# An attention and routed-expert kernel on one core: P transposes on 64-row tiles, wider copies out of PSUM, output scaled on GpSimd

## The chip, the cores and the metric

The kernel runs on one NeuronCore of a Trainium2 chip. The core has five engines that run side by side, each through its own instructions in order: TensorE (PE in the profile, with PEld for the loads of its stationary operand), VectorE (DVE), ScalarE (ACT), GpSimd (POOL) and SyncE (SP, which here issues most of the DMAs). TensorE writes to PSUM, an accumulator memory that DVE and ACT read; GpSimd works on SBUF in this kernel. The metric is the device time of one execution in microseconds. A profiled execution gives a span from the first to the last instruction and the time of each instruction in it.

## The reference, cut to what matters

```python
# q, k, v: 4 batches x 8 heads x 576 positions x 64, float32
scores = 0.125 * q @ k.T
thresh = max(scores, axis=-1) - tau
scores = where(scores >= thresh, scores, -1e9)
attn = exp(scores - max(scores)); attn /= attn.sum(-1) + 1e-9
x = (attn @ v) rearranged to 2304 tokens x 512
# then two layers on the tokens
gate, expert = softmax and argmax of cosine(x, expert_emb) / tau_moe     # 8 experts
x = gate * (relu(x @ w1[expert]) @ w2[expert])                          # 512 -> 1024 -> 512
h = x @ w_in; out = (h * tanh(softplus(h))) @ w_out                     # 512 -> 2048 -> 512
```

Only the attention part is touched by the change; the two layers behind it take two thirds of the time.

## The kernel before, in words

A planner (class `Plan`) takes every piece of work with an engine, a duration, what it reads and writes, and a priority, and writes out one order for each engine. The priorities are sums of a piece's place in the loop and of numbers in the table `PR` (line 34). The order is fixed when the kernel is built; at run time each engine goes through its own list and waits on semaphores.

The attention runs over 16 pairs of heads. For a pair, `scores` makes nine units: unit u = 0 to 7 holds 128 queries of one head against 576 keys, unit 8 holds the last 64 queries of both heads. A unit goes PE (L502), row maximum on DVE (L506), threshold on POOL (L507), exponential on ACT (L508), then mask, product and row sum on DVE (L509), which writes P to SBUF. The scores have a contraction of 64, so each unit uses the array as two tiles of 64 rows and 128 columns: keys 0 to 287 on the upper rows, 288 to 575 on the lower ones, each into its own PSUM bank.

`transp` turns P around for the second product. For each of nine key tiles c of 128 keys, four transposes of 128x128 (L526) fill one PSUM bank, and ACT copies the bank to SBUF (L532, 512 columns). `transp_last` does the same for unit 8 (five transposes at L545, one copy of 640 columns at L548). `pv` multiplies with V in five steps a = 0 to 4 (L561); V is the stationary operand, 64 columns wide, so that the two heads use the two column halves of the array at the same time. Step 4 takes key tile 4, which holds keys of both heads, 64 rows each, on four tiles of 64x64. ACT copies the sum to `osb` (L572, L573); PE turns it back (L583, 5 transposes of 128x128) and forms the logits (L585, 5 products with 16 columns of the matrix `EB`); DVE scales both by the reciprocal row sum and writes `xs` and `xl` to SBUF (L589, L590). After four pairs a batch is done and `router` runs: small DVE steps, a rank by PE (L646 to L649), five squared sums on ACT (`junk`, L675), writes of x to DRAM.

All of this shares four PSUM tiles of two banks each, named D (`two`, line 279): a unit of scores holds one from PE's first product until DVE's L509 is through, two key tiles share one, and the output of `pv` (called `ox` in the code) holds one from the first step until its scaled form is out.

Near the end of the attention `early` picks the largest expert from the first three batches (L714 on PE, then DVE, then L744), so that its weights and its first two tiles of tokens can be fetched (POOL L955) before the last batch is routed. The expert stage follows (L1017 turns the fetched tokens, L1041 and L1059 multiply), then the last layer (L1255, L1283).

## Time and profile before

| | us |
|---|---|
| median of 3 runs | 1044.64 (1043.76 to 1044.7) |
| the profiled execution, own time | 1041.71 |
| its span | 1039.8 |
| PE busy | 987.2 (95%) |
| PEld busy | 797.9 (77%) |
| DVE busy | 757.5 (73%) |
| ACT busy | 548.2 (53%) |
| POOL busy | 321.3 (31%) |
| mean granted TensorE clock | 0.973 of full speed |

The span falls into stages with different limits, so the shares above are averages over unlike things. The attention takes the first third. The columns of the views that follow: a stretch of the windows view gives, for each engine, the time busy and in brackets the number of instructions, then the granted TensorE clock, the share of the DMA engines and GB/s. A row of the timeline gives start, length, engine, line, operation, output<-inputs, shape (rows x columns of the array, then the operand) and count, with idle time and its releaser in square brackets. Matmuls overlap each other, so the length of a row holds the latency of its last one; the distance from one row's start to the next row's start is what the engine took. An fp32 product has two records in the trace, a transpose has one.

### The profile page before, as it was taken

The numbers are of one execution on the slowest core, as the hardware profiler recorded it, in microseconds if no ns is written. First come the engines' busy times: TensorE is split into PE (matmuls) and PEld (weight loads), VectorE is DVE, ScalarE is ACT, GpSimd is POOL, SyncE is SP. The second block draws the span as 40 slices with busy tenths as digits, with TensorE's granted clock in tenths as the row PEclk, the third lists the DMA queues.
The fourth block names the chain that finished last, engine by engine and source line by source line (L and its number), as shares of the span: only waits on it lengthen the run. The fifth ranks groups of instructions, "written<-read, shape, count | busy, mean of one in ns | idle before, by whom it ended". The sixth has DMA issues, their size and how long they took to land. (4 is left out here: it accounts for less than half of the span.)

```text
span 1039.8 us, 16987 instructions
## 1 busy us (share of the span) xinstructions
PE 987.2 (95%) x6381; PEld 797.9 (77%) x6381; DVE 757.5 (73%) x1104; ACT 548.2 (53%) x932; POOL 321.3 (31%) x446
## 2 busy tenths in 40 slices
PE   6999999999898979999999978999999999999996
PEld 3555655655565869899999867998999989899985
DVE  6787887887775858566777859978586866758670
ACT  3666766766654535445566536563544545354440
POOL 4222222212211232322441637423333232422341
PEclk7999999999999789999999988999999999999999
DMA  8222321322313787677799563001000010100000
GB/s 256 82 69 73 119 84 59 119 77 65 100 39 105 264 285 273 234 266 254 266 319 340 185 212 127 22 11 31 22 21 31 22 31 11 32 21 1 22 20 21
DMA packets 41818, 119.28 MB, mean 115 GB/s; under 512 B 8768, under 2 KB 8768, under 8 KB 37632
## 3 DMA queue, kind: packets, MB, share of 16 engines
q1 hardware_dynamic: 37168, 103.13, 29.7%
q0 software_dynamic: 4560, 14.99, 4.4%
q8 instruction: 52, 0.85, 0.4%
q14 instruction: 38, 0.31, 0.1%
HBM read 91.04 MB, written 27.06 MB: 114 GB/s over the span
## 5 line engine op out<-in xcount | busy, mean ns | idle before, releaser
L1273 DVE RECIPROCAL b<-p 128x512 f32<-128x512 f32 x72 | 239.3, 3339 | 18.4 <-ACT p L1270 17.1
L506 DVE TENSOR_REDUCE m<-D 128x1 f32<-128x576 f32 x144 | 107.3, 755 | 50.1 <-PE D L502 48.0
L1276 POOL TENSOR_TENSOR lo<-c,hi 128x512 fp32r<-128x512 f32 x72 | 93.2, 1301 | 139.9 <-ACT hi L1275 133.6
L502 PE MATMUL D<-QK 64*128 64x288 f32 (+1 forms) x640 | 110.8, 468 | 15.1 <-DVE P L509 8.1
L508 ACT ACTIVATE E<-D,m 128x576 f32<-128x576 f32 x144 | 104.7, 745 | 36.5 <-DVE m L506 34.8
L509 DVE SCALAR_TENSOR_TENSOR P<-D,thr,E 128x576 f32<-128x576 f32 x128 | 101.9, 812 | 6.6 <-ACT E L508 3.7
L1268 ACT ACTIVATE p<-S 128x512 f32<-128x512 f32 x72 | 43.0, 598 | 119.3 <-PE S L1255 107.7
L507 POOL TENSOR_SCALAR thr<-m,ntau 128x1 f32<-128x1 f32 x144 | 38.7, 269 | 215.6 <-DVE m L506 193.8
L1274 DVE SCALAR_TENSOR_TENSOR c<-b,S 128x512 f32<-128x512 f32 x72 | 46.4, 658 | 71.0 <-POOL lo L1276 71.0
L1041 PE MATMUL S<-xh,wh 128*128 128x256 f32 (+1 forms) x288 | 89.3, 310 | 0.5 <-ACT xh L1023 0.4
L1041 PE MATMUL S<-xl,wh 128*128 128x256 f32 (+1 forms) x288 | 88.5, 307 | 0.5 <-DVE xl L1024 0.5
L1041 PE MATMUL S<-xh,wl 128*128 128x256 f32 (+1 forms) x288 | 88.3, 307 | 0.0
L526 PE MATMUL D<-ident,P 128*128 128x128 f32 x576 | 84.0, 285 | 2.5 <-ACT hi L532 1.8
L526 PEld LDWEIGHTS D<-ident,P 128*128 128x128 f32 x576 | 63.7, 145 | 28.8 <-issue 10.7
L949 DVE TENSOR_TENSOR wl<-raw,wh 128x1024 fp32r<-128x1024 f32 x49 | 59.4, 1231 | 36.0 <-ACT wh L947 35.5
L1255 PE MATMUL S<-hi,wl 128*128 128x256 f32 x288 | 81.5, 283 | 0.0
L1255 PE MATMUL S<-hi,wh 128*128 128x256 f32 x288 | 81.5, 283 | 0.0
L1255 PE MATMUL S<-lo,wh 128*128 128x256 f32 x288 | 81.4, 283 | 0.0
L561 PE MATMUL D<-hi,V 128*64 128x512 f32 (+1 forms) x160 | 76.5, 616 | 4.0 <-issue 3.8
L1275 ACT CAST hi<-c 128x512 fp32r<-128x512 f32 x72 | 44.1, 618 | 63.6 <-PE B L1283 49.5
L561 PE MATMUL D<-lo,V 128*64 128x512 f32 (+1 forms) x160 | 76.5, 617 | 0.0
L502 PEld LDWEIGHTS D<-QK 64*128 64x128 f32 (+1 forms) x640 | 45.5, 183 | 37.3 <-issue 12.2
(246 smaller groups left out, 2553.1 us busy)
## 6 DMA issues: line engine op xcount, KB each, us to landing
raw<-in_wm_dram SPq DMA_DIRECT2D x32, 1024.0 KB, 6.3
QK<-in_qk_dram SPq DMA_DIRECT2D x32, 432.0 KB, 4.2
fraw<-in_w_in_dram SPq DMA_DIRECT2D x16, 512.0 KB, 6.1
fraw<-in_w_out_dram SPq DMA_DIRECT2D x16, 512.0 KB, 5.2
V<-in_v_dram SPq DMA_DIRECT2D x16, 480.0 KB, 3.4
y_dram<-osb SPq DMA_DIRECT2D x21, 257.0 KB, 5.3
x_dram<-xs SPq DMA_DIRECT2D x16, 256.0 KB, 5.0
w_in_dram<-c SPq DMA_DIRECT2D x16, 256.0 KB, 6.3
```

The source lines that it names most:

```text
L502: nc.tensor.matmul(o, lhsT=QK()[r, a, q0:q0 + w], rhs=QK()[r, a, S:], start=True, stop=True)
L506: add("DVE", 755, lambda: nc.vector.tensor_reduce(m(), sv(), axis=AX.XY, op=ALU.max, negate=True), r=[sc], w=[m], prio=at + PR["max"])
L508: add("ACT", 755, lambda: nc.scalar.activation(Ev(), sv(), AF.Exp, bias=m(), scale=1.0), r=[sc, m], w=[E], prio=at + PR["exp"])
L509: add("DVE", 893, lambda: nc.vector.scalar_tensor_tensor(outs[0]().rearrange("p (a b) -> p a b", a=2), sv(), thr(), Ev(), op0=ALU.is_ge, o ...
L526: pd(nc.tensor.transpose(pt()[:, i * 128:(i + 1) * 128], Ps[i]()[:, c * 128:(c + 1) * 128], self.ident))
L561: mul = lambda j, o, r, c, rhs: nc.tensor.matmul(o, lhsT=V1()[r, c, :], rhs=rhs, start=(a == 0), stop=(a == 4))
L949: add(le, d, lambda: e.tensor_tensor(lo()[:, s], raw()[:, s], hi()[:, s].bitcast(F32), op=ALU.subtract), r=[kr, kh], w=[kl], prio=prio + .5)
L1041: hd(nc.tensor.matmul(hp().rearrange("p (k n) -> p k n", n=128), lhsT=a()[:, kc, f], rhs=x()[:, k0:k0 + n, kc * 128:(kc + 1) * 128], start ...
L1255: hd(nc.tensor.matmul(hp()[:, f * 256:(f + 1) * 256], lhsT=w, rhs=x, start=(n == 0), stop=(n == 11)))
L1273: add("DVE", 3270, lambda q_=q_, r_=r_: v.reciprocal(r_(), g2(q_)), r=[q_], w=[r_], prio=au + R["rc"])
L1274: add("DVE", t_dve(512), lambda gg=gg, r_=r_, hp=hp, hd=hd: hd(v.scalar_tensor_tensor(gg(), r_(), -0.5, hp(), op0=ALU.add, op1=ALU.mult)), ...
L1276: add("POOL", t_pool(512), lambda gg=gg, gh=gh, gl=gl: g.tensor_tensor(g2(gl), gg(), g2(gh).bitcast(F32), op=ALU.subtract), r=[gg, gh], w= ...
```

## The change

1. P's transposes use 64-row tiles. A 128x128 block of P becomes two transposes of 64 rows by 128 columns, upper and lower half of the queries, each into its own PSUM bank: the same two row tiles that the scores use. The transposes of unit 8, those of the output and the logit products are split in the same way.
2. Two key tiles c share one PSUM tile of two banks and one ACT copy of 1024 columns takes both out; the ninth key tile has a copy of 512. A pair then has five such copies instead of nine.
3. V has 16 key tiles instead of 15, padded with zeros, so that step 4 of `pv` uses full 128 rows like the others; its load grows from 480 KB to 512 KB.
4. The scaled output: ACT copies the turned output and the logits from PSUM to a new SBUF tile `xt` (720 columns), and POOL does the two multiplications by the reciprocal row sum. DVE's L589 and L590 go.
5. T (the turned P) and V move to the pool `a_early`, the expert stage's hi and lo rows to the pool `m`.
6. The table `PR` has new numbers, and the planner adds a duration when PE changes between kinds of tiles (`cut`, `SWITCH`). So the order on every engine is another.

```diff
+SWITCH, T_TR, T_LG = 170, 380, 1000
...
+                    if e == "PE" and self.cuts[i] != cut:
+                        t += SWITCH
...
-        V1 = h("a_late", "V1", [128, 15, D], F32, 2, t0 - 9)
+        V1 = h("a_early", "V1", [128, 16, D], F32, 2, t0 - 9)
...
-        T = [self.transp(p, c, Ps) for c in range(9)]
+        T = [self.transp(p, b, Ps) for b in range(5)]
...
-                pd(nc.tensor.transpose(pt()[:, i * 128:(i + 1) * 128], Ps[i]()[:, c * 128:(c + 1) * 128], self.ident))
...
+            for x, c in enumerate(cs):
+                for i in range(4):
+                    for n in range(2):
+                        r = slice(64 * n, 64 * n + 64)
+                        nc.tensor.transpose(pt()[:, n, 256 * x + 64 * i:256 * x + 64 * i + 64], Ps[i]()[r, c * 128:(c + 1) * 128], self.ident[r, r])
...
+        add("ACT", (2 * w + 172) / 1.2, lambda: nc.scalar.copy(T()[:, :, 0:w], pt()[:, :, 0:w]), r=[pt], w=[T], prio=at + PR["Tc"])
...
+                    mul(j, o[j][:, 0, :], a + 5 * j, T[cs[j] // 2]()[:, :, cs[j] % 2 * 256:cs[j] % 2 * 256 + 256])
...
-            nc.vector.tensor_tensor(xs()[:, :, 128 * hp:128 * hp + 128].rearrange("p i (j d) -> p i j d", d=D), flat()[:, 0:640].rearrange("p (i j d) -> p i j d", i=5, j=2), r(D), op=ALU.mult)
-            nc.vector.tensor_tensor(xl()[:, :, 2 * hp:2 * hp + 2, :], flat()[:, 640:720].rearrange("p (i j e) -> p i j e", i=5, j=2), r(NE), op=ALU.mult)
...
+            nc.gpsimd.tensor_tensor(o, i, rd().rearrange("p i j -> p j i").unsqueeze(3).to_broadcast([128, 2, 5, w]), op=ALU.mult)
...
+        add("ACT", 760, lambda: nc.scalar.copy(xt(), ox()[:, :, 0:360]), r=[(ox, 0), (ox, 1)], w=[xt], prio=at2 + PR["xev"])
```

How the order moves. First TensorE in the middle of the attention. Before, from one unit 8 (64x288) on; L502 are scores, L526 transposes of P, L561 products with V:

```order
L502 MATMUL D<-QK 64x288 x4
L561 MATMUL D<-lo,V_2357 64x512
L561 MATMUL D<-hi,V_2357 64x512
L561 MATMUL D<-TL,V_2357 64x64 x2
L526 MATMUL D<-ident,P 128x128 x8
L502 MATMUL D<-QK 128x288 x2
L561 MATMUL D<-hi,V_2357 64x512
L561 MATMUL D<-lo,V_2357 64x512
L561 MATMUL D<-TL,V_2357 64x64 x2
L502 MATMUL D<-QK 128x288 x2
L526 MATMUL D<-ident,P 128x128 x8
```

The kind of tile changes at nearly every step: 18 to 20 times between two units 8, over the whole attention. After, in the same place (the lines stand 5 higher, L531 are transposes, L565 products with V):

```order
L507 MATMUL D<-QK 64x288 x4
L507 MATMUL D<-QK 128x288 x2
L565 MATMUL D<-T,V_1484 64x512 x2
L565 MATMUL D<-TL,V_1484 64x64 x2
L565 MATMUL D<-T,V_1484 64x512 x2
L565 MATMUL D<-TL,V_1484 64x64 x2
L531 MATMUL D<-ident,P 128x64 x24
L507 MATMUL D<-QK 128x288 x4
L565 MATMUL D<-T,V_1484 64x512 x2
L565 MATMUL D<-TL,V_1484 64x64 x2
L531 MATMUL D<-ident,P 128x64 x16
```

Products with V stand in groups of two, two and one steps, and scores and transposes, now of one kind, stand next to each other: the kind changes 8 times between two units 8.

GpSimd in the same stretch, before (L459 scales the keys, L507 is the threshold):

```order
L459 TENSOR_SCALAR QK<-QK 128x288
L507 TENSOR_SCALAR thr<-m,ntau 128x1
L459 TENSOR_SCALAR QK<-QK 128x288
L507 TENSOR_SCALAR thr<-m,ntau 128x1 x9
L459 TENSOR_SCALAR QK<-QK 128x288
```

After (L593 scales the output, L512 is the threshold):

```order
L464 TENSOR_SCALAR QK<-QK 128x288 x2
L512 TENSOR_SCALAR thr<-m,ntau 128x1 x3
L593 TENSOR_TENSOR xs<-xt,rd 128x2x5x64
L512 TENSOR_SCALAR thr<-m,ntau 128x1
L593 TENSOR_TENSOR xl<-xt,rd 128x2x5x8
L512 TENSOR_SCALAR thr<-m,ntau 128x1 x5
```

Each pair has two multiplications more, with one threshold between them.

TensorE at the end of the attention, before (L714 is the count from which the first expert is chosen, L583 and L585 belong to the pair before the last, V_4792 to the last pair):

```order
L561 MATMUL D<-TL,V_4792 64x64 x2
L714 MATMUL D<-run_128,ones 128x8
L583 MATMUL D<-ident,osb 128x128 x5
L585 MATMUL D<-EB,osb 128x16 x5
L561 MATMUL D<-hi,V_4792 64x512
L561 MATMUL D<-lo,V_4792 64x512
```

After (L719 is the count; L585 and L588 are the last pair's; V_5267 is the last pair's V; L651 to L654 rank a batch):

```order
L565 MATMUL D<-T,V_5267 64x512 x2
L565 MATMUL D<-TL,V_5267 64x64 x2
L651 MATMUL D<-run_126,ones 128x40
L653 MATMUL D<-oh,ones 128x32
L653 MATMUL D<-oh,ones 128x24
L653 MATMUL D<-oh,ones 128x16
L653 MATMUL D<-oh,ones 128x8
L654 MATMUL D<-oh,tri 128x40
L719 MATMUL D<-run_128,ones 128x8
L585 MATMUL D<-ident,osb 128x64 x10
L588 MATMUL D<-EB,osb 128x8 x10
```

The count now stands behind all products with V and behind a batch's rank. From the experts' first products on, TensorE's list is the same in both but for the place of eight transposes of tokens.

## Rows read from the trace of the kernel before

**Rows 1.** Windows by stage, cut at unit 8 of pairs 0, 13, 15 and L1041
```profile
17.89:268.60 250.71, 242.55 (x1727) 142.92 (x1727) 202.09 (x456) 165.89 (x294) 58.34 (x146) 0.98 0.29 88
268.60:313.67 45.07, 41.28 (x298) 25.70 (x297) 35.05 (x90) 27.56 (x51) 8.20 (x21) 0.96 0.24 68
313.67:343.17 29.50, 25.25 (x199) 17.90 (x199) 16.54 (x51) 15.18 (x30) 3.73 (x9) 0.86 0.42 146
343.17:400.00 56.83, 49.05 (x310) 44.35 (x311) 43.18 (x98) 25.03 (x46) 17.71 (x19) 0.89 0.77 264
400.00:1039.80 639.80, 620.76 (x3820) 562.70 (x3818) 451.15 (x387) 307.90 (x504) 223.98 (x204) 0.99 0.32 110
```

**Rows 2.** Groups of DVE, ACT and POOL: count, busy us, mean ns, idle before, releaser
```profile
L506 DVE TENSOR_REDUCE m<-D 128x1 f32<-128x576 f32 x135 | 101.1, 755 | 47.7 <-PE D L502 45.6
L509 DVE SCALAR_TENSOR_TENSOR P<-D,thr,E 128x576 f32<-128x576 f32 x121 | 96.5, 813 | 6.6 <-ACT E L508 3.7 <-ACT lo L532 0.5 <-POOL thr L507 0.3
L589 DVE TENSOR_TENSOR xs<-D,rd 128x640 f32<-128x640 f32 x14 | 11.5, 821 | 0.6 <-PE D L585 0.4
L590 DVE TENSOR_TENSOR xl<-D,rd 128x80 f32<-128x80 f32 x14 | 3.2, 230 | 0.0
L508 ACT ACTIVATE E<-D,m 128x576 f32<-128x576 f32 x134 | 97.7, 745 | 29.0 <-DVE m L506 27.4 <-DVE rd L474 0.7
L532 ACT COPY hi<-D 128x512 f32<-128x512 f32 x67 | 39.3, 587 | 28.3 <-PE D L526 27.8
L548 ACT COPY TL<-D 128x640 f32<-128x640 f32 x15 | 10.4, 693 | 12.3 <-PE D L545 12.3
L1276 POOL TENSOR_TENSOR lo<-c,hi 128x512 fp32r<-128x512 f32 x72 | 93.2, 1301 | 139.9 <-ACT hi L1275 133.6
```

**Rows 3.** Timeline of PE, steps with a change of tile kind between them
```profile
212.08 1.09 PE L526 MATMUL D<-ident,P 128*128 128x128 f32 x8
213.11 0.76 PE L502 MATMUL D<-QK 64*128 64x288 f32 x4
213.79 0.64 PE L561 MATMUL D<-hi,V 128*64 128x512 f32 x1
...
214.92 0.76 PE L502 MATMUL D<-QK 64*128 64x288 f32 x4
```

**Rows 4.** Timeline of PE, steps of one kind that follow each other
```profile
311.91 1.24 PE L502 MATMUL D<-QK 64*128 64x288 f32 x8
313.08 0.65 PE L526 MATMUL D<-ident,P 128*128 128x128 f32 x4
...
315.43 0.59 PE L561 MATMUL D<-lo,V 128*64 128x512 f32 x1
...
316.41 0.59 PE L561 MATMUL D<-hi,V 128*64 128x512 f32 x1
...
317.48 2.84 PE L526 MATMUL D<-ident,P 128*128 128x128 f32 x24
...
320.16 0.71 PE L545 MATMUL D<-ident,PL 128*128 128x128 f32 x5
```

**Rows 5.** Timeline of PEld: loads of the transposes, scores and logit products
```profile
212.08 0.20 PEld L526 LDWEIGHTS D<-ident,P 128*128 128x128 f32 x2
...
213.10 0.30 PEld L502 LDWEIGHTS D<-QK 64*128 64x128 f32 x4 [0.17 <-issue]
...
203.55 1.20 PEld L585 LDWEIGHTS D<-EB,osb 128*128 128x128 f32 x10
```

**Rows 6.** Timeline of PE, the longest stall of the attention
```profile
268.60 0.72 PE L502 MATMUL D<-QK 64*64 64x288 f32 x8
273.08 0.64 PE L561 MATMUL D<-hi,V 128*64 128x512 f32 x1 [3.76 <-issue]
```

**Rows 7.** Timeline of PE, from the count to the experts' first products
```profile
325.48 0.39 PE L714 MATMUL D<-run,ones 128*128 128x8 f32 x2
...
337.35 1.11 PE L1017 MATMUL S<-ident,q 128*128 128x128 f32 x4 [2.48 <-DMA q<-x_dram,ids]
...
343.17 0.58 PE L1041 MATMUL S<-xh,wh 128*128 128x256 f32 x1 [0.45 <-ACT xh L1023]
```

101 lines of the change are left out of this document (49 added, 52 removed).

## The prediction

> **What bounds the kernel now.** I read the stages first, because the change touches only one of them [rows 1]. From unit 8 of the first pair (17.89) to unit 8 of the fourteenth (268.60) lie 13 pairs: 250.71 / 13 = 19.28 us a pair, with PE busy 242.55 of 250.71, DVE 202.09, ACT 165.89, POOL 58.34. Per pair that is PE 18.7, DVE 15.5, ACT 12.8, POOL 4.5. The next two pairs take 45.07, so 45.07 - 2 x 19.28 = 6.5 us more than two plain ones; the end of the attention up to the experts' first product takes 29.50; what follows takes about 697 us and its list on TensorE stays as it was.
>
> A busy PE need not be the bound, since its rows hold latency. So I looked at who waits for whom [rows 2]: DVE's row maximum stood idle 47.7 us, of which 45.6 waited for the scores of PE, while the mask step L509 stood idle 6.6 us only. ACT's copies of P^T waited for PE's transposes, 27.8 us in the one of the two groups shown. Everything waits for PE. The one long stall of PE itself, 3.76 us [rows 6], comes where the first batch-end work sits on ACT and the D tiles stay occupied. The bound of the attention is PE's time per pair.
>
> **The change part by part.**
>
> *Changes of tile kind.* A single unit of scores between other work takes 213.79 - 213.11 = 0.68 us [rows 3], two in a row take 313.08 - 311.91 = 1.17 [rows 4]; so the second takes 0.49, and 0.19 goes with the change of kind: the array runs dry and the first load is not hidden. A step with V takes 316.41 - 315.43 = 0.98 behind another one [rows 4], and 214.92 - 213.79 = 1.13 alone [rows 3]: 0.15. Eight transposes take 213.11 - 212.08 = 1.03 alone [rows 3]; 24 take 320.16 - 317.48 = 2.68 ahead of others of their kind, 0.112 each with the first load, about 0.11 [rows 4]; 1.03 - 8 x 0.11 = 0.15. So a change costs about 0.16 (0.15 to 0.19). The order lists 18 to 20 of them in a pair before and 8 after: 11.5 x 0.16 = 1.85 us a pair (1.7 to 2.2).
>
> *The transposes themselves.* A pair has 36 blocks of P, 5 of unit 8 and 5 of the output: 46 x 0.11 = 5.1 us now. After, each block is two transposes of 64 moving columns on two row tiles. What p does a block cost then? From below: half the columns, 0.055, if the two halves run side by side and their loads hide. For side by side speaks the row of the scores' loads: four loads of 64x128 on the same two row tiles lie in 0.30 us [rows 5]; and a score product passes 288 columns in each of its two records, which at a transpose's pace (0.11 / 128, 0.86 ns a column) is 0.49 us, yet a unit of two such products takes 0.49 in all [rows 4]. For the hiding speaks that two loads of transposes lie within 0.20 us [rows 5], so the second started no more than 0.06 after the first, since one such load takes 0.14. From above: the logit products, which move only 16 columns, go at the pace of their loads, ten in 1.20, 0.11 to 0.12 each [rows 5]; were the new transposes bound like that, p = 0.112 and nothing is gained. I take p = 0.06, since the loads of transposes are the nearer row: 46 x (0.11 - 0.06) = 2.3 us a pair (0 to 2.5).
>
> The Trainium skill (TensorE: Matmul & The Clock Gate, section on LDWEIGHTS) has a rule against this part: a load's time goes with its columns, P / 1.2 ns, and not with its rows. By it each half-height transpose of 128 columns pays the full 107 ns for its load, p is 0.107 and the estimate for this part is 46 x (0.110 - 0.107) = 0.1 us a pair instead of 2.3. The row of the logit loads agrees with it, the row of the transposes' loads [rows 5] is about half of that.
>
> *The logits.* Before, ten passes, each with a load of 128 columns, in 1.20 us [rows 5]; after, twenty on two row tiles, two at a time: the same, 0.
>
> *Step 4 of the products with V* goes on full rows at the width it has now: 0 in time, its changes of kind are counted above. The load of V grows by 32 KB in stretches where the DMA engines are busy 0.24 to 0.29 [rows 1]: 0.
>
> So PE needs 19.28 - 1.85 - 2.3 = 15.1 us a pair at p = 0.06, and 17.4 at p = 0.112.
>
> *DVE* loses 0.821 + 0.230 = 1.05 us a pair [rows 2]: 15.5 - 1.05 = 14.5.
>
> *ACT.* Copies of 512 and 640 columns take 587 and 693 ns [rows 2], so 0.83 ns a column, and one of 1024 about 1.01 us. Nine copies, 5.28 us, become four of 1.01 and one of 0.59, 4.64; the new copy of 720 columns adds 0.76. Sum +0.1: ACT needs 12.9, no bound.
>
> *POOL.* A multiplication of 512 columns takes 1301 ns [rows 2], so 640 columns about 1.6 and 80 about 0.3 us; the strided output is not in the trace, and at double the price they take 3.8. POOL needs 4.5 + 1.9 = 6.4 (8.3 at most), no bound by itself. But behind the long one stand thresholds, and behind a threshold L509. ACT's exponential (0.745) runs while the threshold (in the trace before rarely the last to come: 0.3 us of L509's idle time [rows 2]) is made; a threshold that is late by 1.6 us loses about 0.8 for L509. Since DVE will have slack of its own, I put it at 0 to 0.8 a pair and count it in what follows.
>
> *The D tiles.* The faster PE meets the next limit, four PSUM tiles. A unit holds one for its product 0.5, maximum 0.76, exponential 0.75, mask 0.81 [rows 2] and some 0.4 of handovers, 3.2 us, and 0.75 more on average because three units are served one behind the other: nine take 36. Four of the new transposed tiles hold theirs for 0.5 + 1.0 + 0.3 each, the fifth and that of unit 8 for 1.4: 10. The output holds one nearly all the time now (its steps are spread over the whole pair), which leaves three: 46 / 3 = 15.4 us a pair.
>
> So after the change three demands lie close together: PE 15.1, tiles 15.4, DVE 14.5. Engines that go through fixed lists and wait for each other don't reach the largest of such demands. Before, PE was 3 us ahead of the rest and there was little to lose; I add 1.2 us, the size of one handover chain per pair: **16.6 us a pair**, 2.7 less.
>
> *The last two pairs* keep their 6.5 us of extra work (ranks, ACT's squared sums, the stall of rows 6). 15 pairs x 2.7 = 40 us.
>
> *The end.* 325.48 - 313.67 = 11.8 us lie between unit 8 and the count L714, 343.17 - 325.48 = 17.7 from there to the first expert product [rows 7]. After, the count stands behind all products with V: eight steps (7.8), about 45 transposed blocks (2.7), logits (1.2), two ranks (2.7), changes of kind (1.3), some 16 us behind unit 8. What follows it is a chain: choice, list, fetch by POOL, arrival, 337.35 - 325.48 = 11.9 us, then some 3 of transposes and splitting, 15. So 31 instead of 29.5. Against that, the last batch's scaled output comes about 2 us sooner behind unit 8, although POOL takes 0.9 us more for it than DVE, and the next wait of PE, in the stage up to 400 (busy 49.05 of 56.83 [rows 1]), is for what follows from it. Net I take 1 us gained, between 5 lost and 4 gained. The expert stage moves as a whole.
>
> The sum against the profiled execution's own 1041.7 (span 1039.8 and 1.9 around it): 1041.7 - 40 - 1 = 1000.7. The median of the runs shown, 1044.6, lies 2.9 above that execution; so 1003.5.
>
> **The rivals.**
> 1. *Transposes at the pace of their loads*, p = 0.112: PE 17.4 a pair and, as now, well ahead of the rest. 15 x 1.9 + 1 = 29 us gained: 1015. For it the logit loads, against it the transposes' own loads [rows 5].
> 2. *The D tiles or POOL's thresholds become the bound*, 18 a pair: 15 x 1.3 = 19 gained, 1025. For it: the stall of rows 6 shows that PE does stand still when D tiles are not freed, and the wide copies free two key tiles at once only after 1 us; against it that 15.4 leaves room. The Trainium skill (TensorEngine Tiling (Array Packing), PSUM Bottleneck) warns of this: tiling speeds TensorE but not the evacuation of PSUM. The trace of before agrees in one place only, that stall of 3.76 us.
> 3. *Slower: the two half-height transposes run one after the other.* Then a block costs two passes at the present pace, 0.22: PE 19.28 - 1.85 + 46 x 0.11 = 22.5 a pair, 3.2 more, 15 x 3.2 = 48: 1092. It decides against the change from p = 0.11 + 1.85 / 46 = 0.15 on. Against it stand the scores, whose two products share their time on the same two row tiles [rows 4, 5].
> 4. *It does nothing*: the chain from scores to L509 sets the pace and PE's gain turns into waiting: 1044. Against it DVE's 45.6 us of waiting for PE.
> 5. *Better*: the demands of 15.1 to 15.4 are met and the end gains too: 15 x 4 = 60: 984.
>
> **How the numbers follow.** Forecast 0.44, rival 1 0.25, rival 2 0.12, rival 3 0.06, rival 4 0.03, rival 5 0.10. The range from 986 to 1030 leaves out rival 3 and about half of rival 5, with a little of the others. Runs of this kernel differ by some 0.1%, so about 0.2% (2 us) can be told from no change. Faster 0.91, within that 0.03, slower 0.06.
>
> **What would show it.** In the profile after: unit 8 every 16 to 17 us; 16 half transposes from start to start in about 0.5 us with one copy of about 1 us behind them (0.9 us would be rival 1, 1.8 rival 3); a unit of scores 0.5 us wherever it follows transposes; DVE's idle time before the maximum smaller and that before L509 larger than 6.6; if L509 waits mostly for POOL, rival 2. The forecast is wrong if PE still has no waits and pairs of 17.4 or more, or if PE waits in every pair for D tiles.

## The result, and the profile after

The changed kernel takes 1010.39 us (median of 4 runs, 1007.20 to 1017.09) where the kernel before takes 1044.2 on the same chip (4 runs, 1040.52 to 1044.7): a ratio of 0.969, 95% interval 0.964 to 0.975. The forecast was 1003.5 with a range from 986 to 1030, so sign and range were right and the centre was 7 us too low. The profiled execution of after has an own time of 1008.81 and a span of 1007.1 us (before: 1041.71 and 1039.8). Lines of the code stand 5 higher than before.

The stages of after, by windows cut at the same places as [rows 1]: unit 8 of pairs 0, 13 and 15, the first expert product (now L1046), 400:

```profile
18.84:236.81 217.97, 203.83 (x2437) 125.08 (x2438) 185.46 (x427) 167.71 (x252) 77.45 (x170) 0.98 0.34 105
236.81:271.32 34.51, 32.70 (x399) 20.57 (x397) 28.28 (x66) 25.20 (x38) 9.68 (x24) 1.00 0.21 65
271.32:315.50 44.18, 27.75 (x307) 19.72 (x306) 27.56 (x95) 22.43 (x44) 10.17 (x14) 0.75 0.38 113
315.50:400.00 84.50, 80.08 (x474) 73.60 (x471) 56.34 (x101) 39.32 (x65) 23.96 (x27) 0.95 0.80 282
400.00:1007.10 607.10, 588.07 (x3641) 532.35 (x3640) 430.05 (x359) 291.11 (x480) 213.82 (x195) 0.98 0.29 100
```

Three things are to be seen. The first 13 pairs take 217.97 instead of 250.71 and the next two 34.51 instead of 45.07: from unit 8 of the first pair to unit 8 of the last, 252.48 instead of 295.78, **43.3 us gained**. The end of the attention takes 44.18 instead of 29.50, and TensorE is busy for only 27.75 of it at a granted clock of 0.75: 14.7 lost. From the first expert product to the first product of the last layer, which starts at 570.95 (before: 604.22), it is 255.4 instead of 261.0. So from the last unit 8 to the last layer **9.1 us are lost**, 299.6 against 290.6. The first unit 8 comes 0.95 later and the last layer takes 0.6 longer: 43.3 - 0.95 - 9.1 - 0.6 = 32.7, which is the difference of the spans.

The plain pairs of after take 16.31 us each: unit 8 stands at 136.33, 152.64 and 168.95. The two at a batch's end take 19.20 and 18.94, each with 3.4 us at a granted clock of 0.50 in it (from 112.8 and from 181.1). Before, plain pairs took 18.53 and 19.87 in turn; the 13 pairs of [rows 1], batch ends with them, took 19.28 on average. One plain pair of after in the columns of the windows:

```profile
136.33:152.64 16.31, 15.62 (x194) 9.57 (x193) 13.67 (x30) 12.51 (x19) 5.77 (x13) 1.00 0.27 88
```

Groups of the attention in after, with the columns of [rows 2]:

```profile
L511 DVE TENSOR_REDUCE m<-D 128x1 f32<-128x576 f32 x144 | 104.0, 753 | 25.6 <-PE D L507 24.9
L514 DVE SCALAR_TENSOR_TENSOR P<-D,thr,E 128x576 f32<-128x576 f32 x128 | 100.3, 811 | 12.9 <-ACT E L513 12.3 <-issue 0.2
L534 ACT COPY T<-D 128x1024 f32<-128x1024 f32 x64 | 65.0, 1017 | 23.6 <-PE D L531 23.1
L593 POOL TENSOR_TENSOR xs<-xt,rd 128x640 f32<-128x640 f32 x16 | 20.3, 1270 | 33.8 <-ACT xt L596 33.8
L596 ACT COPY xt<-D 128x720 f32<-128x720 f32 x16 | 12.0, 751 | 2.7 <-PE D L588 2.7
L593 POOL TENSOR_TENSOR xl<-xt,rd 128x80 f32<-128x80 f32 x16 | 5.2, 328 | 0.0
```

VectorE's wait for scores has halved, from 47.7 to 25.6 us, and its wait ahead of the mask step has doubled, from 6.6 to 12.9, most of it now for the exponential and none of it named for GpSimd. The wide copy takes 1.02 us, GpSimd's two multiplications 1.27 and 0.33.

TensorE in the middle of the attention, in the form of [rows 3] and [rows 4]:

```profile
186.70 0.72 PE L531 MATMUL D<-ident,P 64*128 64x64 f32 x16
187.25 2.07 PE L507 MATMUL D<-QK 64*128 64x288 f32 x16
189.25 1.08 PE L565 MATMUL D<-T,V 128*64 128x512 f32 x4
...
196.00 0.76 PE L507 MATMUL D<-QK 64*128 64x288 f32 x4 [0.45 <-DVE P L514]
196.56 0.50 PE L585 MATMUL D<-ident,osb 64*128 64x64 f32 x10
196.87 1.26 PE L588 MATMUL D<-EB,osb 64*128 64x8 f32 x20
197.96 0.54 PE L549 MATMUL D<-ident,PL 64*128 64x64 f32 x10
...
199.09 0.71 PE L531 MATMUL D<-ident,P 64*128 64x64 f32 x16
199.64 1.19 PE L507 MATMUL D<-QK 64*128 64x288 f32 x8
```

Sixteen half transposes, which are eight blocks of P, take 187.25 - 186.70 = 0.55 us from start to start; the eight full ones of [rows 3] took 1.03. Twenty-four that wait for nothing take 0.80 at the full clock (L531, 286.22 to 287.02), so a block costs (0.80 - 0.55) / 4 = 0.0625. Four units of scores take 189.25 - 187.25 = 2.00, 0.50 each. A single one between transposes of its own kind, at 196.00, takes 0.56 where a single one took 0.68 to 0.69 before. The 0.45 in its brackets is the only wait of TensorE that this view names in a plain pair of after.

The end of the attention on TensorE, in the form of [rows 7] (L719 is the count, L588 the last logits, L749 the first fetch list, L653 the last batch's rank, L1022 the fetched tokens, L827 the lists, L1046 the experts' first products):

```profile
275.40 0.64 PE L565 MATMUL D<-T,V 128*64 128x512 f32 x1 [2.36 <-ACT T L534]
...
292.93 0.37 PE L719 MATMUL D<-run,ones 128*128 128x8 f32 x2
293.23 0.53 PE L585 MATMUL D<-ident,osb 64*128 64x64 f32 x10
293.59 1.23 PE L588 MATMUL D<-EB,osb 64*128 64x8 f32 x20
297.82 0.56 PE L749 MATMUL D<-M,A 128*128 128x4 bf16 x15 [3.00 <-DVE M L742]
...
300.63 1.88 PE L653 MATMUL B<-oh,ones 128*128 128x32 f32 x8 [1.75 <-DVE oh L635]
...
306.81 2.25 PE L1022 MATMUL S<-ident,q 128*128 128x128 f32 x8 [3.45 <-DMA q<-x_dram,ids]
314.80 0.88 PE L827 MATMUL B<-xs,A 128*128 128x42 bf16 x20 [5.73 <-DVE xs L819]
315.50 0.56 PE L1046 MATMUL S<-xh,wh 128*128 128x256 f32 x1
319.08 0.58 PE L1046 MATMUL S<-xl,wh 128*128 128x256 f32 x1 [3.02 <-DVE xl L1029]
```

From 293.6 on TensorE waits for something at almost every step. Its granted clock there:

```profile
293.59:297.13 3.54, 1.23 (x26) 1.14 (x22) 3.27 (x12) 0.78 (x2) 1.37 (x2) 1.00 0.05 9
297.13:324.44 27.31, 12.61 (x83) 11.31 (x84) 21.85 (x76) 11.07 (x21) 7.82 (x11) 0.50 0.91 306
324.44:342.00 17.56, 17.56 (x117) 16.13 (x117) 9.59 (x17) 7.33 (x14) 4.98 (x6) 1.00 0.83 316
```

Behind a stretch with TensorE busy for 1.23 of 3.54 us the granted clock lies at 0.50, its lower level of 1.2 GHz, for 27.3 us. Before, the same place had 13.7 us at that level, from 335.0 on.

### The profile page after: what moved, and what is told of

It is laid out like the page before. It is cut to its first block, busy times and chain, and to the rows that moved or that the text cites. A ratio compares the mean times of both kernels' runs of the same rounds, so it can differ in the third digit from the quotient of the medians.

```text
span 1007.1 us, 18782 instructions
## 1 busy us (share of the span) xinstructions
PE 942.0 (94%) x7277; PEld 776.0 (77%) x7277; DVE 737.5 (73%) x1072; ACT 552.6 (55%) x884; POOL 344.3 (34%) x477
## 5 line engine op out<-in xcount | busy, mean ns | idle before, releaser
L507 PE MATMUL D<-QK 64*128 64x288 f32 (+1 forms) x640 | 105.3, 462 | 20.8 <-DVE P L514 12.1
L511 DVE TENSOR_REDUCE m<-D 128x1 f32<-128x576 f32 x144 | 104.0, 753 | 25.6 <-PE D L507 24.9
L513 ACT ACTIVATE E<-D,m 128x576 f32<-128x576 f32 x144 | 101.2, 742 | 34.2 <-DVE m L511 30.7
L514 DVE SCALAR_TENSOR_TENSOR P<-D,thr,E 128x576 f32<-128x576 f32 x128 | 100.3, 811 | 12.9 <-ACT E L513 12.3
L534 ACT COPY T<-D 128x1024 f32<-128x1024 f32 (+1 forms) x80 | 74.2, 931 | 36.4 <-PE D L531 35.9
L1046 PE MATMUL S<-xl,wh 128*128 128x256 f32 (+1 forms) x288 | 87.9, 305 | 3.0 <-DVE xl L1029 3.0
L1046 PE MATMUL S<-xh,wh 128*128 128x256 f32 (+1 forms) x288 | 88.7, 308 | 0.0
L1046 PE MATMUL S<-xh,wl 128*128 128x256 f32 (+1 forms) x288 | 87.8, 305 | 0.0
L565 PE MATMUL D<-T,V 128*64 128x512 f32 x320 | 84.6, 610 | 3.3 <-ACT T L534 2.4
L507 PEld LDWEIGHTS D<-QK 64*128 64x128 f32 (+1 forms) x640 | 51.4, 190 | 44.2 <-issue 18.3
L512 POOL TENSOR_SCALAR thr<-m,ntau 128x1 f32<-128x1 f32 x144 | 38.0, 264 | 131.6 <-DVE m L511 116.8
L954 DVE TENSOR_TENSOR wl<-raw,wh 128x1024 fp32r<-128x1024 f32 x49 | 59.3, 1231 | 30.2 <-ACT wh L952 30.0
L952 ACT CAST wh<-raw 128x1024 fp32r<-128x1024 f32 x64 | 63.8, 1045 | 11.2 <-PE B L1064 6.1
L1064 PE MATMUL B<-wh,lo 128*128 128x512 f32 x168 | 65.8, 391 | 1.1 <-DVE lo L1052 1.1
```

The costliest lines, as they stand in the source:

```text
L507: nc.tensor.matmul(o, lhsT=QK()[r, a, q0:q0 + w], rhs=QK()[r, a, S:], start=True, stop=True)
L511: add("DVE", 755, lambda: nc.vector.tensor_reduce(m(), sv(), axis=AX.XY, op=ALU.max, negate=True), r=[sc], w=[m], prio=at + PR["max"])
L513: add("ACT", 755, lambda: nc.scalar.activation(Ev(), sv(), AF.Exp, bias=m(), scale=1.0), r=[sc, m], w=[E], prio=at + PR["exp"])
L514: add("DVE", 893, lambda: nc.vector.scalar_tensor_tensor(outs[0]().rearrange("p (a b) -> p a b", a=2), sv(), thr(), Ev(), op0=ALU.is_ge, o ...
L534: add("ACT", (2 * w + 172) / 1.2, lambda: nc.scalar.copy(T()[:, :, 0:w], pt()[:, :, 0:w]), r=[pt], w=[T], prio=at + PR["Tc"])
L565: mul = lambda j, o, c, rhs: nc.tensor.matmul(o, lhsT=V1()[:, c, :], rhs=rhs, start=(a == 0), stop=(a == 4))
```

## The experiments

Twelve kernels were run. "Pace" is the distance from one unit 8 to the next in the plain pairs, "attention" that from the first unit 8 to the last, "to the last layer" from the last unit 8 to the first product of the last layer; all are read from the timeline of TensorE of the profiled execution. The times of before, after, t2, t4 and no_switch are medians of four or more runs, the others are one run each. The kernels ran on several chips, on which before took 1042.3 (one run) to 1044.3.

| kernel | time | pace | attention | to first expert product | to the last layer |
|---|---|---|---|---|---|
| before | 1044.2 | 18.5, 19.9 | 295.8 | 29.5 | 290.6 |
| after | 1010.4 | 16.31 | 252.5 | 44.2 | 299.6 |
| e_full | 1025.7 | 17.45 | 266.7 | 46.2 | 302.3 |
| e_dve_scale | 1015.2 | 16.57 | 258.6 | 44.3 | 300.2 |
| e_two_copies | 1006.4 | 16.43 | 251.4 | 44.2 | 298.1 |
| o1 | 1035.4 | 18.1 to 18.9 | 287.3 | 33.6 | 294.2 |
| s_pe | 1016.3 | 16.99 | 260.6 | 45.4 | 300.1 |
| s_dve | 1021.0 | 17.06 | 265.2 | 42.9 | 298.0 |
| s_pool | 1012.9 | 16.55 | 257.1 | 45.3 | 299.4 |
| b_pe | 1057.2 | 19.41, 20.75 | 310.1 | 30.4 | 292.5 |
| b_dve | 1049.7 | 18.54, 19.88 | 299.7 | 29.5 | 293.1 |
| t2 | 1009.7 | 16.3 | 264.0 | 28.4 | 293.1 |
| t4 | 1006.8 | 16.3 | 260.6 | 21.3 | 291.2 |
| no_switch | 1010.8 | 16.76 | 258.5 | 33.0 | 296.1 |

### What bounded the pairs before

**b_pe**, the kernel before with 8 of P's 36 blocks transposed twice:

```diff
-            for i in range(4):
+            for i in list(range(4)) * (2 if c in (0, 5) else 1):
```

> The kernel before, with the transposes of key tiles 0 and 5 made twice in every pair: 8 blocks of 128x128 more on TensorE, 8 x 0.11 = 0.87 us a pair, in the same order and between the same neighbours. The prediction's reading (TensorE bounds the pairs of before alone): the pace goes from 19.2 to 20.0-20.2 us a pair, and 16 pairs make the kernel about 13 us longer, near 1055. Rival (waits and engines bound it together, as they do in the changed kernel, where 1.0 us more on TensorE cost 0.68): no more than 0.6 a pair, 1051 or less.

The pairs go from 18.53 to 19.41 and from 19.87 to 20.75: +0.88 in each, where 0.87 us of work was added. Added work on TensorE shows up whole, so the reading that TensorE bounded the pairs holds, and the 0.11 us of a full block with it (0.88 / 8). A short pair of b_pe, and the one wait that every second pair of before has:

```profile
57.78:77.19 19.41, 19.41 (x145) 11.97 (x144) 14.66 (x33) 11.86 (x20) 3.95 (x11) 1.00 0.22 72
```

```profile
170.32 0.76 PE L502 MATMUL D<-QK 64*128 64x288 f32 x4 [1.00 <-DVE P L509]
```

In the short pairs TensorE has no idle time at all. In the long ones it waits 1.0 us for VectorE's mask step, which frees a D tile, so there "everything waits for PE" is not the whole of it; that wait is 1.01 in b_pe and 1.01 in b_dve, so neither addition fills or lengthens it.

**b_dve**, the kernel before with four more small steps of VectorE, 0.84 us a pair:

```diff
+                for _ in range(4):
+                    nc.vector.tensor_scalar(rd(), den, 1e-9, None, op0=ALU.add)
```

> The kernel before, with four more small steps of VectorE on the row sums of each pair, 0.84 us a pair on VectorE and nothing else; in the changed kernel the same steps cost 0.75 us a pair. The prediction's reading (VectorE stood idle 3.5 us a pair, waiting for scores): pace +0 to +0.2 us a pair, time within 3 us of before (1041 to 1047). Rival (VectorE is already next to the bound): +0.4 or more a pair, 1050 or more.

The plain pairs stay at 18.54 and 19.88, within 0.01 of before. The first pair, those at a batch's end and one more are 0.8 to 1.1 longer, 3.9 in all. The time of this one run, 1049.7, is outside the 1041 to 1047 of the theory and next to the 1050 of the rival; 2.5 us of that lie behind the attention, where nothing was changed, and 0.9 ahead of the first unit 8, and they stay unexplained. On the pace, which it was made for, the rival of a VectorE next to the bound falls.

### What bounds them after

**s_pe**, the changed kernel with the transposes of four key tiles made twice, 16 blocks or 1.0 us a pair at 0.0625:

```diff
-            for x, c in enumerate(cs):
+            for x, c in list(enumerate(cs)) * (2 if b in (0, 2) else 1):
```

> The changed kernel with four of the nine key tiles' transposes made twice (the same result written again), 16 blocks at 0.062, 1.0 us a pair more on TensorE. If TensorE alone sets the pace: units 8 every 17.3 us instead of 16.3. If DVE or the D tiles set it: 16.5 or less. Theory (demands close together): 16.7 to 17.1.

**s_dve**, the changed kernel with the same four steps of VectorE as b_dve, 0.84 us a pair:

> The changed kernel with four repeated small steps on DVE ahead of the reciprocal of each pair, about 0.2 us each, 0.8 us a pair more on DVE. If DVE sets the pace: units 8 every 17.1 us instead of 16.3. If TensorE alone: 16.3. Theory (demands close together): 16.5 to 16.9.

**s_pool**, the changed kernel with GpSimd's long multiplication made twice, 1.3 us a pair:

```diff
+            for _ in range(2 if w == D else 1):
-            nc.gpsimd.tensor_tensor(o, i, rd().rearrange("p i j -> p j i").unsqueeze(3).to_broadcast([128, 2, 5, w]), op=ALU.mult)
+                nc.gpsimd.tensor_tensor(o, i, rd().rearrange("p i j -> p j i").unsqueeze(3).to_broadcast([128, 2, 5, w]), op=ALU.mult)
```

> The changed kernel, with GpSimd's multiplication of 640 columns made twice: about 1.3 us a pair more on GpSimd, all of it ahead of the thresholds that follow. If GpSimd has room and the thresholds behind it are covered by the exponential, pace +0 to +0.15, time 1009 to 1012. Rival (the thresholds behind the multiplication hold up the mask step, as rival 2 of the prediction has it): +0.5 or more a pair, 1018 or more.

The same kind of edit, so much work for so much pace, gives: TensorE +0.68 for 1.0, VectorE +0.75 for 0.84, GpSimd +0.24 for 1.3. (Five of the plain pairs of s_pe are slower, 17.2 to 17.6. Over all 15 distances the three are +0.54, +0.85 and +0.31 a pair.) Before it was +0.88 for 0.87 on TensorE and 0 on VectorE. So after the change no engine alone is the bound: VectorE, which had slack to spare, now passes on nine tenths of what is added to it, and TensorE two thirds. s_pe came out as the theory had it. s_dve did not: 17.06 lies above its 16.5 to 16.9 and at the 17.1 put down for VectorE alone, which the 16.99 of s_pe speaks against in turn. The trace shows how both can be. The lone unit of scores that waits 0.45 for the mask step in after (the row at 196.00) waits in s_dve:

```profile
169.59 0.76 PE L509 MATMUL D<-QK 64*128 64x288 f32 x4 [1.20 <-DVE P L516]
```

The 0.75 more in this wait are the 0.75 of pace, while TensorE's busy time stays at 15.62 a pair. So the two engines meet at one point of the order in each pair, where TensorE needs a D tile that VectorE frees; VectorE is busy for only 13.67 of 16.31 and is no bound by its sum. GpSimd's result lies between the two expectations: it is no bound, but not free either. The group of the mask step in s_pool shows where its 0.24 come from, a wait for the threshold that the changed kernel doesn't have (2.6 us in 12 waits, 0.22 each):

```profile
L514 DVE SCALAR_TENSOR_TENSOR P<-D,thr,E 128x576 f32<-128x576 f32 x128 | 100.4, 812 | 15.6 <-ACT E L513 12.3 <-POOL thr L512 2.6 <-issue 0.2
```

### What each part of the change is worth

**e_full**, the changed kernel with the 36 blocks of P on full rows again; one copy for two key tiles and the numbers of the plan as in after. A key tile then fills one PSUM bank instead of half of two, and the copies and products with V that read it follow (not shown):

```diff
-                    for n in range(2):
-                        r = slice(64 * n, 64 * n + 64)
-                        nc.tensor.transpose(pt()[:, n, 256 * x + 64 * i:256 * x + 64 * i + 64], Ps[i]()[r, c * 128:(c + 1) * 128], self.ident[r, r])
+                    nc.tensor.transpose(pt()[:, x, 128 * i:128 * i + 128], Ps[i]()[:, c * 128:(c + 1) * 128], self.ident)
```

> The changed kernel with the 36 blocks of P transposed on full 128 rows again, in the same places of the order, two key tiles to a PSUM tile and one copy as changed. Theory (TensorE's time counts): a block costs 0.109 instead of 0.062 us, 36 x 0.047 = 1.7 us a pair, and transposes no longer share the scores' kind of tile, some 7 more changes at 0.16, 1.1 us: units 8 every 18 to 19 us instead of 16.3, the attention 25 to 42 us longer. Rival (D tiles or DVE set the pace): at most 0.5 us a pair, under 8 us.

The time rises by 15 us, the pace by 1.14, between the two expectations. TensorE's timeline:

```profile
190.78 1.09 PE L529 MATMUL D<-ident,P 128*128 128x128 f32 x8
191.80 1.24 PE L507 MATMUL D<-QK 64*128 64x288 f32 x8
192.97 1.08 PE L563 MATMUL D<-T,V 128*64 128x512 f32 x4
...
196.09 2.09 PE L507 MATMUL D<-QK 64*128 64x288 f32 x16
198.11 1.08 PE L563 MATMUL D<-T,V 128*64 128x512 f32 x4
```

Eight full blocks take 191.80 - 190.78 = 1.02, against 0.55 in after. So the half height is worth 36 x (0.11 - 0.0625) = 1.7 us of TensorE a pair. A plain pair:

```profile
125.95:143.40 17.45, 17.30 (x158) 10.82 (x156) 13.65 (x30) 12.54 (x19) 5.81 (x13) 1.00 0.25 83
```

TensorE is busy for 17.30 of 17.45, 1.68 more than the 15.62 of after, and has no wait for VectorE left: 0.54 of the 1.68 went into idle time that after has, and 1.14 into the pace. With full transposes TensorE would be the bound of the changed kernel again. The scores behind full transposes take 2.02 for four units and 1.17 for two; in after, behind half transposes, 2.00 and 1.15 to 1.18 where no wait is in between. So going from transposes to scores costs next to nothing when several units stand together. What a group of full transposes has on top of its blocks is 1.02 - 8 x 0.11 = 0.14, the half ones 0.55 - 8 x 0.0625 = 0.05.

**e_dve_scale**, the output scaled by VectorE from PSUM again, without the copy `xt`:

```diff
-            nc.gpsimd.tensor_tensor(o, i, rd().rearrange("p i j -> p j i").unsqueeze(3).to_broadcast([128, 2, 5, w]), op=ALU.mult)
+            nc.vector.tensor_tensor(o, i, rd().rearrange("p i j -> p j i").unsqueeze(3).to_broadcast([128, 2, 5, w]), op=ALU.mult)
...
-        add("ACT", 760, lambda: nc.scalar.copy(xt(), ox()[:, :, 0:360]), r=[(ox, 0), (ox, 1)], w=[xt], prio=at2 + PR["xev"])
```

> The changed kernel with the scaling of the output on DVE straight from PSUM, as it was before the change. DVE gets about 1.05 us a pair more, ACT 0.76 and POOL 1.6 less. Theory (three demands close together, DVE one of them): units 8 every 16.5 to 17.2 us instead of 16.3. Rival (thresholds queued behind POOL's long multiplication cost DVE time): 16.0 or less.

Pace +0.26. VectorE gets 1.05 us a pair back, as the forecast priced it:

```profile
L592 DVE TENSOR_TENSOR xs<-D,rd 128x640 f32<-128x640 f32 x15 | 12.4, 824 | 12.6 <-PE D L588 12.6
L592 DVE TENSOR_TENSOR xl<-D,rd 128x80 f32<-128x80 f32 x15 | 3.5, 230 | 0.0
```

It costs less than the answer of s_dve (0.9 for 1.0) would give. The order on VectorE is another, and ACT and GpSimd are relieved; which of these makes the difference was not tested. Over all 15 distances, with the pairs at a batch's end, it is 6.1 us, 0.4 a pair. So the move to GpSimd is worth 0.3 to 0.4 us a pair, as the theory of this run had it, and its rival falls.

**e_two_copies**, ACT copies the two key tiles one by one, 512 columns each:

```diff
+            for x in range(len(cs)):
+                nc.scalar.copy(T()[:, :, 256 * x:256 * x + 256], pt()[:, :, 256 * x:256 * x + 256])
```

> The changed kernel with two ACT copies of 512 columns for each transposed PSUM tile instead of one of 1024. ACT gets 4 x 0.16 = 0.6 us a pair more by the rows of before, and a tile is held 0.1 to 0.2 us longer. Theory: ACT is no bound, the pace moves by 0 to 0.2 us a pair, 0 to 3 us in all. Rival (the wide copy is where the gain is): 0.6 us a pair, 9 us.

Pace +0.12; the time of the one run, 1006.4, lies 0.8 under the fastest run of after, on a chip where the one run of before took 1042.3, and the attention is 1.1 shorter. No gain of the wide copy shows.

**o1**, the changed kernel's operations with the kernel before's values for the numbers in `PR` that both tables have:

```diff
-'S': -49.15, 'max': -410.56, 'Tp': 135.0, 'po': -11.3, 'px': 265.78, 'xev': 254.09
+'S': -20.53, 'max': 31.56, 'Tp': -21.15, 'po': 64.5, 'px': 55.38, 'xev': 14.53
```

> The changed kernel with the numbers of the table PR from before, so only the order differs: the planner then sets 5 changes of tile kind between two units 8 instead of 8. Theory (changes cost 0.16 each): TensorE needs 0.5 us a pair less, and if it alone sets the pace, units 8 come every 15.8 us. Rival (the spacing of scores and transposes over the D tiles sets the pace): 17 us or more, with TensorE waiting for DVE.

1035.4: with its operations alone the change gains 7 us on the kernel before of that chip (1042.3), in one run each; the attention is 8.5 us shorter than before. The kind of tile changes 5 times a pair here, less than the 8 of after; in three pairs at full clock TensorE is busy for 15.2 us, 0.4 less than in after. Still the pace is 18.1 to 18.9. Busy time in the stretch from 60 to 240, and the longest of TensorE's waits in it (us in total, times, longest):

```profile
60.00:240.00 180.00, 153.60 (x1874) 93.70 (x1870) 138.20 (x321) 126.57 (x197) 59.23 (x128) 0.96 0.28 89
...
PE D L507 <- ACT T L534: 12.2, 9, 1.6
```

TensorE is busy for 153.6 of 180 us (in after 170.2). Nine times the scores wait for ACT's copy of the turned P, because D tiles are not free: many transposes in a row take tiles that the next scores need. The rival of this run holds in its pace and in the D tiles, but TensorE waits less for VectorE, as it had it (6.0 and 3.4 us), than for that copy. It is what rival 2 of the prediction describes, and the order decides whether it happens: in the same stretch of after the scores have no such wait. So fewer changes of kind pay only with an order that spaces the D tiles; which of the numbers that differ does the spacing was not separated. What the new numbers would do for the old operations was not tried on the chip.

### Where the end lost what it lost

**t2** takes two numbers of before, which give the ranks' tiles and with them the count an earlier place; **t4** goes further and puts the count right behind the last unit 8:

```diff
-'rkpos': 98.03, 'rkpos2': 33.29
+'rkpos': 57.24, 'rkpos2': 23.07
```

> The changed kernel with two numbers of the table PR taken from before (rkpos, rkpos2): the count stands ahead of the last three steps of products with V, the lists of the last batch behind 36 expert products. Theory: the place of the count and of the lists is what the end lost, so the first product comes 34 to 38 us behind the last unit 8 instead of 44, the run is 6 to 9 us faster than the changed kernel's. Rival: no change beyond 2 us.

```diff
-'ep': 107.77, 'ep2': 1508.23, 'rkpos': 98.03, 'rkpos2': 33.29
+'ep': 8.0, 'ep2': 5.0, 'rkpos': 40.0, 'rkpos2': 20.0
```

> The changed kernel with four numbers of the table PR changed (rkpos 40, rkpos2 20, ep 8, ep2 5), which place the ranks and the count of the first expert earlier: the count stands right behind the last unit 8, its list behind four steps of products with V, and the lists of the last batch stand behind the first 60 expert products. The pairs keep their order. In the changed kernel 21.6 us pass from the last unit 8 to the count and 22.6 from there to the first expert product (before: 11.8 and 17.7). Theory (the late count and the lists ahead of the first products lose the 10 us that the end lost): the first product comes 24 to 30 us behind unit 8 instead of 44, the run is 10 to 18 us faster than the changed kernel's, 992 to 1000. Rival (the chain of the last batch sets the end): the first product comes earlier, but the last layer starts less than 5 us earlier.

**no_switch** keeps all numbers and sets the planner's price for a change of kind to zero:

```diff
-SWITCH, T_TR, T_LG = 170, 380, 1000
+SWITCH, T_TR, T_LG = 0, 380, 1000
```

> The changed kernel, with the planner's price for a change of tile kind set to zero; all other numbers stay. Its order keeps 8 changes in each plain pair, but at the end of the attention the count of the first three batches stands ahead of the last three steps with V instead of behind them, and the lists' 20 products stand behind the first 48 products of the experts instead of ahead of them. Theory (the expert stage is tied to the last batch's lists, not to its own first product): pace 16.3 and sum 251 to 254 as in the changed kernel, the first expert product 3 to 8 us earlier, but the last layer starts within 3 us of where it did when both are counted from unit 8 of the last pair (299.6 us behind it); 1005 to 1011. Rival (the late count cost the 14.7 us that the end lost): the last layer starts earlier by what the first product gains, 5 us or more, 1003 or less. If the planner's price is what groups the kinds, the pace is 17 or more; the order speaks against that already.

t2 takes 1009.7 (ratio 0.966, 0.964 to 0.969), t4 1006.8 (0.963, 0.960 to 0.965), no_switch 1010.8 (0.967, 0.965 to 0.970). The interval of after, 0.964 to 0.975, overlaps with each, so none is shown to be faster than it, and the 6 to 9 us of t2's theory and the 10 to 18 of t4's are missed. In t4 the first expert product comes 14.6 us earlier than in after (300.90 against 315.50), and the last layer starts at the same time (570.84 against 570.95): the rival holds. What the start of the last layer goes with is the time of the lists of all tokens, which need the last batch's ranks:

| us | before | after | t2 | t4 | no_switch |
|---|---|---|---|---|---|
| from the last unit 8 to the lists (L822, L827) | 38.3 | 43.5 | 35.9 | 35.7 | 42.5 |
| the first expert product ahead of the lists | 8.8 | -0.7 | 7.5 | 14.4 | 9.5 |
| from the lists to the last layer | 252.3 | 256.2 | 257.1 | 255.5 | 253.6 |

The lead of the first product varies by 15 us, the time from the lists to the last layer by 5, and the largest lead doesn't go with the shortest time. That the lists bind the stage is read from this table; no run moved them alone. In t4 TensorE starts early and then waits, behind the lists, for tokens to be fetched:

```profile
315.31 0.73 PE L827 MATMUL B<-xs,A 128*128 128x42 bf16 x20 [2.80 <-DVE xs L819]
336.77 1.09 PE L1022 MATMUL S<-ident,q 128*128 128x128 f32 x4 [3.08 <-DMA q<-x_dram,ids]
```

t4 and t2 reach the lists 7.8 and 7.5 us sooner behind the last unit 8 than after does, and the last layer 8.4 and 6.6 sooner. Against that, their pairs are 8.1 and 11.5 us longer in sum, though t4's expectation said that the pairs keep their order: ranks now stand between the scores (distances of up to 21.4 us in t4, 20.6 in t2). So in these two the end's loss seems to have moved into the pairs; what each of the longer pairs waits for was not followed up.

no_switch tells two things more. Its first product gains 11.2 us against after (33.0 behind the last unit 8 instead of 44.2) and its last layer 3.5, which is 0.5 more than the theory allowed and far from the 5 or more of the rival. And its order has the same 8 changes of kind in a plain pair, so the planner's price isn't what groups them; the numbers are. The pace is 16.76 all the same, a miss of both expectations. The output's transposes stand one step further ahead; over the pairs GpSimd's multiplication waits 42.3 us for `xt`, where it waits 15.8 in after, and the loads of the scores wait 18.1 us for the mask step, 2.7 in after. Which of these makes the pace was not tested.

## Why the prediction was right, and where it was off

**The bound.** Read rightly in the main. b_pe passes TensorE's added work on whole, b_dve doesn't pass VectorE's on in plain pairs. What the prediction didn't see is the wait of 1.0 us for VectorE in every second pair of before: it took the whole 19.28 as TensorE's need, where TensorE is busy for 18.5 and 18.8 in plain pairs.

**Changes of kind.** Their size was right: in the trace of before a step with V alone takes 1.12 and the second of two 0.98, and a lone unit of scores 0.69 against 0.48 to 0.50 in a row; in after four units take 2.00. Their number fell as the order said. What the 1.85 us a pair are worth by themselves was not measured: o1 has fewer changes still and is slow. The nearest is e_full, where 13 changes are left of 19 to 20: TensorE is busy for 17.30 there instead of 18.7, 1.4 less, of which 10 x (0.11 - 0.0625) = 0.5 are the blocks of unit 8 and of the output. That leaves 0.9 for six to seven changes, 0.14 each.

**The transposes.** p was taken as 0.06, between bounds of 0.055 and 0.112; it is 0.0625 by the rows of the P blocks, so the term is 46 x (0.11 - 0.0625) = 2.2 instead of 2.3, and rival 1 (0.112) and rival 3 (0.22) fall with it. The deciding row was the right one: the loads of the transposes themselves in [rows 5], not those of the logits. By an estimate from the rule of the Trainium skill (TensorE: Matmul & The Clock Gate, section on LDWEIGHTS) p would have been 0.107; the trace of after disagrees, since two half-height transposes, each with a load of 128 columns, pass in 0.0625. For the logits its rule stays in agreement with the rows: twenty half-height products, two at a time, take 197.96 - 196.87 = 1.09 us, against 1.20 for ten before, so the forecast of 0 was nearly right there.

**VectorE, ACT, GpSimd.** 1.05 us off VectorE (0.824 + 0.230 in e_dve_scale); the wide copy 1.02 against 1.01 forecast; `xt` 0.75 against 0.76. GpSimd's long multiplication takes 1.27, not 1.6: the price per column taken from L1276 was too high for it. The delay of thresholds, put at 0 to 0.8 a pair, was near 0: of the idle time ahead of the mask step none is put down to them.

**The three close demands and the pace.** Forecast 16.6 a pair from PE 15.1, tiles 15.4, DVE 14.5 and 1.2 for their interplay; measured 16.31. In a plain pair (136.33 to 152.64) TensorE is busy for 15.62 of 16.31 and VectorE for 13.67. TensorE's need was put 0.5 too low: the two terms add up to 4.0, its busy time fell by 3.1 (18.7 to 15.6; such rows hold some latency). What comes on top of it is 0.7, of which 0.45 is the one wait for VectorE, and not 1.5. So the two errors cancel, and that the pace came out within 0.3 is in part luck. s_pe and s_dve show that TensorE and VectorE do hold each other up, as said, but through that one wait. The D tiles as a limit over the whole pair showed in o1 and not in after. The warning of the Trainium skill (TensorEngine Tiling (Array Packing), PSUM Bottleneck) that tiling speeds TensorE but not the evacuation of PSUM agrees with o1, where the scores wait 12.2 us for copies of T; in the same stretch of after they have no such wait.

**The pairs as a whole** gained 43.3 where 40 was forecast. The 6.5 us that the last two pairs had extra became 34.51 - 2 x 16.31 = 1.9, and two pairs at the ends of batches now have 2.9 and 2.6 extra: the batch-end work moved and was not lost, as the prediction had it.

**The end is the step that failed.** It said "Net I take 1 us gained, between 5 lost and 4 gained", and 9.1 were lost. Two terms of it can be read off. The count was put "some 16 us behind unit 8" and came 292.93 - 271.32 = 21.6 behind it: the first two steps with V, from 271.96 to 278.25, took 6.3 us instead of 2.1 (2.36 of them a wait for a copy of T, and the granted clock was at 0.50 from 276.6 to 280.0), and the 33 transposed blocks behind them 3.3 instead of 2.1; the rest of the list took what was put down for it. And "3 of transposes and splitting, 15" from the count to the first product became 22.6. Of these 7.6, 2.0 lie ahead of the fetched tokens' transposes (306.81 - 292.93 = 13.9 where 11.9 were put) and 5.6 behind them: there TensorE waits 5.73 for the lists, which VectorE makes. VectorE, which I left out of this sum, does the choice, the last batch's rank and the splitting one behind the other. Before, the choice ran while TensorE still had four steps with V and two outputs to do. VectorE's rows, first of before, then of after (L717 and L722 begin the choice, L625 and L630 the rank, L949 and L954 split weights):

```profile
325.90 0.17 DVE L717 TENSOR_REDUCE most<-D 128x1 f32<-128x8 f32 x1 [5.87 <-PE D L714]
...
334.01 2.36 DVE L949 TENSOR_TENSOR wl<-raw,wh 128x1024 fp32r<-128x1024 f32 x2 [4.29 <-ACT wh L947]
...
337.29 0.74 DVE L625 TENSOR_REDUCE rt<-xl 128x40 f32<-128x320 f32 x1
```

```profile
294.09 0.16 DVE L722 TENSOR_REDUCE most<-D 128x1 f32<-128x8 f32 x1
...
298.69 0.72 DVE L630 TENSOR_REDUCE rt<-xl 128x40 f32<-128x320 f32 x1
...
306.04 2.35 DVE L954 TENSOR_TENSOR wl<-raw,wh 128x1024 fp32r<-128x1024 f32 x2
...
311.28 2.35 DVE L954 TENSOR_TENSOR wl<-raw,wh 128x1024 fp32r<-128x1024 f32 x2
```

Before, 11.4 us and a wait of 4.3 lie between the beginnings of choice and rank. In after 4.6 us lie between them, with a wait of 0.3 only: the rank starts when the choice is through, though its input `xl` was ready at 297.36, 1.3 earlier. And then the splitting of weights, 2 x 2.35 us, stands between the rank and the lists on VectorE; before it was two single ones of 1.22 there. The way from the last unit 8 to the lists, step by step:

| us | before | after | t4 |
|---|---|---|---|
| to the last pair's logits (L585, L588) | 20.0 | 22.3 | 17.2 |
| from there to the last rank's products (L648, L653) | 5.6 | 7.0 | 8.1 |
| from there to the lists (L822, L827) | 12.7 | 14.2 | 10.4 |
| sum | 38.3 | 43.5 | 35.7 |

So the sentence that the last batch's scaled output comes "about 2 us sooner behind unit 8" was wrong too: its logits came 2.3 later. These 5.2 us and the 3.9 between the lists and the last layer make the 9.1. For the 3.9 the clock is a candidate: the lower level holds for 9.6 us behind the lists of after (314.80 to 324.44) and for 6.8 in before. But t2 and t4 have 10.2 us each there and end 1.0 over and 0.6 under after. Over all fourteen kernels, the four with under 7 us at the lower level there (before, b_pe, o1, no_switch) take 252.3 to 253.6 from the lists to the last layer, the ten with 7.6 or more 254.4 to 257.1, which speaks for the clock and doesn't show it; it stays open.

**What I overlooked.** The part on the change says that from the experts' first products on TensorE's list is the same but for eight transposes. It isn't: the 20 products of the lists, which stood behind the first expert products (L822 at 351.98, 8.8 us behind L1041), stand ahead of them in after (L827 at 314.80, 0.7 ahead of L1046). The first product then waits for the lists, though what it reads was there 5.8 us earlier: its weights were ready and the tokens `xh` of both tiles at 309.7, by the first of these rows.

```profile
309.10 0.58 ACT L1028 CAST xh<-S 128x512 fp32r<-128x512 f32 x1 [0.34 <-PE S L1022]
```

```profile
318.35 0.68 DVE L1029 TENSOR_TENSOR xl<-S,xh 128x512 fp32r<-128x512 f32 x1
```

But the second product, at 319.08, waits for an `xl` that VectorE makes at 318.35, so a first product ahead of the lists would have gained little by itself unless VectorE's order had changed too. I had looked at where the count went and not at who else passed it. no_switch, where the lists stand behind 48 expert products again, the count stands ahead of three steps with V and VectorE's order is another, shows what all this together is worth: the first product comes 11.2 us sooner, the last layer 3.5. What the place of the lists alone costs was not measured.

**The rivals.** None of the five happened. Rival 2 was a right mechanism that o1 shows; rival 5 had both too good, the pairs (4 us each, measured about 2.9) and the end.

The sum in one line, against the profiled execution: 1000.7 forecast, -3.3 for the pairs, +0.95 for the first unit 8, +10.1 for the end (9.1 lost where 1 was to be gained), +0.6 for the last layer, -0.2 for what lies outside the span: 1008.8. The runs of before differ by more than the 0.1% that the prediction took: 1040.52 to 1044.7, 0.4%. The gain of 34 us is far beyond that.

## What to carry to other kernels

When one engine is the bound and its row is near 100% busy, price the change on that engine by distances from start to start of the same instruction in the trace, and then ask for the next engine's slack: here 3 us a pair came off before the second one held it up, and a small experiment that adds 0.8 us to one engine, read together with the one wait that grows by it, tells which it is better than busy shares do. Where a table of numbers sets the order, a new table is a change of its own, and under the old one the new operations brought 7 us of 34, in one run each; follow every instruction that it moves past another, on every engine of the path, up to the point where the next stage is really released (here the lists, not the first product).
